# A job planner with an engine model in place of a hand-timed order, and PSUM banks given out job by job, in a fused attention and MLP-mixer kernel

## The chip, the cores and the metric

The kernel runs on one core of a Trainium2 chip. The metric is the device time of one execution in microseconds (us). A run is marked slow when it is over 1.5% above the fastest run of the same kernel, and such runs are left out of every ratio. A ratio is the mean time of one kernel's fast runs over the mean of the other's fast runs of the same rounds, so it is not quite the ratio of the medians that are quoted beside it. Brackets behind a ratio are its 95% interval.

The engines are PE (matrix multiply; PEld is its weight load), DVE (vector), ACT (activation), POOL (general) and SP, which here only issues transfers (its timelines in the traces of before and after list 60 issues each and nothing else). PE writes its results to PSUM, which this kernel uses as eight banks of 128 partitions by 512 float32. Other work that takes a bank waits until ACT or DVE has read it out: in the trace of the kernel before, PE waited for that 27 times at the attention's matmuls, 16.8 us in all.

## The reference

The inputs are drawn as float32. There are 8 batches and 8 heads, the sequence length is 1024, the head size 64.

```python
k_proj = np.einsum('ks,bhsd->bhkd', E, k)           # 1024 keys projected to 64
v_proj = np.einsum('ks,bhsd->bhkd', F, v)
attn   = softmax(q @ k_proj^T / sqrt(64))
x      = heads side by side of attn @ v_proj        # (8, 1024, 512)
# MLP-mixer:
h   = np.maximum(x^T @ w_tok1, 0) @ w_tok2          # token mixing, 1024 -> 256 -> 1024
u   = x + h^T
out = u + np.maximum(u @ w_ch1, 0) @ w_ch2          # channel mixing, 512 -> 1536 -> 512
```

(The softmax is written out in the reference, with the largest score subtracted.) Both kernels compute in bfloat16 with float32 sums.

## The kernel before

The work of a batch has two parts. The **front** is attention and token mixing: project k and v, transpose q, scores, exp on ACT, attention times v, then two token products and a transpose of u. The **channel mixing** handles each batch as two **sub-blocks** of 512 rows, 16 sub-blocks in all. It uses a seven-product scheme in the manner of Strassen for each 2 by 2 block product. A sub-block has three **up** sets of seven products of four matmuls, and one **down** block of seven products of twelve matmuls, all of 256 columns. The front of the next batch is woven between the channel products of the current one.

Each PSUM bank is a tile of its own here, from three rotating pools: three banks for up, three for down, two for the front.

```python
psU = ctx.enter_context(tc.tile_pool(name="psU", bufs=3, space=bass.MemoryType.PSUM))
psD = ctx.enter_context(tc.tile_pool(name="psD", bufs=3, space=bass.MemoryType.PSUM))
psF = ctx.enter_context(tc.tile_pool(name="psF", bufs=2, space=bass.MemoryType.PSUM))
```

The attention of a head is done in two halves, of one front bank each:

```python
def attend(b, h, half):
    o_ps = psF.tile([P, 4, D1], F32, tag="f", name="o_ps")
    for jj in range(2):
        ...                                              # one matmul of 130 columns
    rdn = attn_pool.tile([P, 4], F32, tag="rdn", name="rdn")
    nc.vector.reciprocal(out=rdn, in_=o_ps[:, :, D])
    nc.vector.tensor_tensor(
        out=xs[b][:, 4 * half : 4 * half + 4, h * D : (h + 1) * D],
        in0=o_ps[:, :, 0:D], in1=rdn[:, :, None].to_broadcast([P, 4, D]), op=ALU.mult)
```

The order comes from a list of events with times chosen by hand. All events are sorted by time and emitted in that order, and `pin()` keeps it. Note the first unit of a front, which is the place where the q transposes of the batch are issued:

```python
def front(b, begin, end):
    unit(0.0, lambda: (start_front(b), q_transpose(b)))   # two DMA transposes on SP
    unit(1.9, lambda: kv_proj(b, 0, H))
    ...
    unit(0.4, lambda: scores(0))
    if b + 1 < B:
        unit(0.0, lambda: load(b + 1, "q_sb", q, 2))      # POOL: waits until qT has read q_sb
    ...                                                   # scores, attend, token1, token2
front(1, 26, 45)
for b in range(2, B):
    front(b, 42 * b - 46 + OFF, 42 * b - 4 + OFF)
...
for _, _, f in sorted(events, key=lambda e: e[:2]):
    f()
    pin()
```

SP issues three things in the order of the program: the DMA transposes of q (qT), the DMA transposes of u (uT), and the output stores. An issue whose input is not ready holds up everything behind it: in the trace of the kernel before, one pair of uT held the queue for 20.16 us, and the store and the qT pair behind it were issued 0.1 and 0.7 us after its end.

The softmax here doesn't subtract the row's maximum and nothing guards it: scores larger than these inputs give would overflow.

Of the kernel before, what the change touches and what calls it, by code (L numbers as in the profile page):

```python
# [13 lines left out]
FMAX = 3.4028234663852886e38  # L14


@with_exitstack
def kernel(
# [13 lines left out]
    nc = tc.nc  # L32
# [36 lines left out]
    const = ctx.enter_context(tc.tile_pool(name="const", bufs=1))  # L69
    one = ctx.enter_context(tc.tile_pool(name="one", bufs=1))  # L70
    two = ctx.enter_context(tc.tile_pool(name="two", bufs=2))
    attn_pool = ctx.enter_context(tc.tile_pool(name="attn", bufs=4))
    out_pool = ctx.enter_context(tc.tile_pool(name="outp", bufs=3))
    psU = ctx.enter_context(tc.tile_pool(name="psU", bufs=3, space=bass.MemoryType.PSUM))
    psD = ctx.enter_context(tc.tile_pool(name="psD", bufs=3, space=bass.MemoryType.PSUM))
    psF = ctx.enter_context(tc.tile_pool(name="psF", bufs=2, space=bass.MemoryType.PSUM))

    seen[0] = len(nc.cur_bb.bb.instructions)

    ident = const.tile([P, P], BF16, name="ident")  # L80
    make_identity(nc, ident)
    E_sb = out_pool.tile([P, S], BF16, tag="o", name="E_sb")
    nc.gpsimd.dma_start(out=E_sb[:KP], in_=E)
    F_sb = out_pool.tile([P, S], BF16, tag="o", name="F_sb")
    nc.gpsimd.dma_start(out=F_sb[:KP], in_=F)

    loaded = {}

    def load(b, name, src, parts):
        if (b, name) not in loaded:  # L90
            loaded[b, name] = one.tile([P, H, NSI, D], BF16, tag=name, name=name)
        hn = H // parts
        for h in range(0, H, hn):
            nc.gpsimd.dma_start(
                out=loaded[b, name][:, h : h + hn],
                in_=src[b, h : h + hn].rearrange("h (p si) d -> p h si d", p=P),
            )

    for name in ("k_sb", "v_sb", "q_sb"):
        loaded[0, name] = one.tile([P, H, NSI, D], BF16, tag=name, name=name)  # L100

    def load_pair(name, src, hp):
        hs = slice(2 * hp, 2 * hp + 2)
        nc.gpsimd.dma_start(
            out=loaded[0, name][:, hs], in_=src[0, hs].rearrange("h (p si) d -> p h si d", p=P)
        )

    for hp in range(HP):
        load_pair("k_sb", k, hp)
        load_pair("v_sb", v, hp)  # L110
    for hp in range(HP):
        load_pair("q_sb", q, hp)

    wt1_sb = const.tile([P, NSI, DT], BF16, name="wt1_sb")
    nc.gpsimd.dma_start(out=wt1_sb, in_=moe_w_tok1.rearrange("(p si) t -> p si t", p=P))
    wt2_sb = const.tile([P, TC, S], BF16, name="wt2_sb")
    nc.gpsimd.dma_start(out=wt2_sb, in_=moe_w_tok2.rearrange("(tc p) s -> p tc s", p=P))

    wc1_sb = const.tile([P, 2, 2, 2, DC // 2], BF16, name="wc1_sb")
    w1_v = moe_w_ch1.rearrange("(dc p) (ch c) -> p dc ch c", p=P, ch=2)  # L120
    cw = DC // 2 // SETS
    for m in range(SETS):
        cs = slice(m * cw, (m + 1) * cw)
        for ch in range(2):
            nc.gpsimd.dma_start(
                out=wc1_sb[:, :, :, ch, cs].rearrange("p a b c -> p (a b) c"),
                in_=w1_v[:, :, ch, cs],
            )

    wc2_sb = const.tile([P, 2, C2, DM], BF16, name="wc2_sb")  # L130
    w2_v = moe_w_ch2.rearrange("(ch cc p) d -> p ch cc d", ch=2, p=P)
    for ch in range(2):
        for c in range(0, C2, 3):
            nc.gpsimd.dma_start(out=wc2_sb[:, ch, c : c + 3], in_=w2_v[:, ch, c : c + 3])


    wT1 = const.tile([P, 3, 2, DC // 2], BF16, name="wT1")
    wT2 = const.tile([P, 3, C2, DH], BF16, name="wT2")
    load(1, "k_sb", k, 2)
    load(1, "v_sb", v, 2)  # L140
    load(1, "q_sb", q, 2)

# [13 lines left out]
    def combine2(c):  # L156
        cs = slice(c, c + 3)
        combine(
            [wT2[:, n, cs] for n in range(3)],
            *(wc2_sb[:, ch, cs, dh * DH : (dh + 1) * DH] for ch in range(2) for dh in range(2)),  # L160
        )



    vb = const.tile([P, H, 2, D1], BF16, name="vb")
    kT = const.tile([P, H, 2, KP], BF16, name="kT")
    nc.vector.memset(vb, 0.0)
    nc.vector.memset(kT, 0.0)
    for half in range(2):
        nc.vector.memset(vb[half * KP : (half + 1) * KP, :, half, D:D1], 1.0)  # L170
    zero = const.tile([P, P], BF16, name="zero")
    nc.vector.memset(zero, 0.0)

    ET_sb = const.tile([P, NSI, KP], BF16, name="ET_sb")
    FT_sb = const.tile([P, NSI, KP], BF16, name="FT_sb")
    for src, dst in ((E_sb, ET_sb), (F_sb, FT_sb)):
        e_ps = psF.tile([P, NSI, KP], BF16, tag="f", name="e_ps")
        for si in range(NSI):
            nc.tensor.transpose(e_ps[:, si, :], src[:KP, si:S:NSI], ident[:KP, :KP])
        nc.vector.tensor_copy(out=dst, in_=e_ps)  # L180
    pin()

    xs, us, uTs, Ss, Gs = {}, {}, {}, {}, {}
    st = {}


    def start_front(b):
        xs[b] = one.tile([P, NSI, DM], BF16, tag="x_sb", name="x_sb")
        us[b] = two.tile([P, NSI, DM], BF16, tag="u_sb", name="u_sb")
        st["hT"] = one.tile([P, TC, DM], BF16, tag="hT_sb", name="hT_sb")  # L190
        st["qT"] = one.tile([P, H, NJ, P], BF16, tag="qT", name="qT")
        st["kp"] = one.tile([KP, H, 2, D], BF16, tag="kp_sb", name="kp_sb")

    def start_uT(b, i):
        uTs[2 * b + i] = two.tile([P, NJ, DMC, P], BF16, tag="uT", name="uT")

    def q_transpose(b):
        for h in range(0, H, H // 2):
            nc.sync.dma_start_transpose(
                out=st["qT"][:, h : h + H // 2].rearrange("p h j s -> p (h j) s"),  # L200
                in_=loaded[b, "q_sb"][:, h : h + H // 2].rearrange("p h si d -> p (h si d)"),
            )

    def q_transpose_pe(hp):
        t_ps = psU.tile([P, 2, NJ, P], BF16, tag="u", name="t_ps")
        for h in range(2):
            for j in range(NJ):
                nc.tensor.transpose(
                    t_ps[:, h, j, :],
                    loaded[0, "q_sb"][:, 2 * hp + h, 2 * j : 2 * j + 2, :].rearrange(  # L210
                        "p s d -> p (s d)"
                    ),
                    ident,
                )
        nc.vector.tensor_copy(out=st["qT"][:, 2 * hp : 2 * hp + 2], in_=t_ps)

    def kv_proj(b, h0, hn, pool=None):
        k_sb, v_sb = loaded[b, "k_sb"], loaded[b, "v_sb"]
        hs = slice(h0, h0 + hn)
        kv_ps = psF.tile([P, H, D], F32, tag="f", name="kv_ps")  # L220
        for si in range(NSI):
            a, z = si == 0, si == NSI - 1
            nc.tensor.matmul(
                kv_ps[0:KP, 0:hn], ET_sb[:, si, :], k_sb[:, hs, si, :], start=a, stop=z
            )
            nc.tensor.matmul(
                kv_ps[KP : 2 * KP, 0:hn], FT_sb[:, si, :], v_sb[:, hs, si, :], start=a, stop=z
            )
        kp = st["kp"]
        nc.vector.tensor_copy(out=kp[:, hs, 0, :], in_=kv_ps[0:KP, 0:hn])  # L230
        nc.scalar.copy(out=kp[:, hs, 1, :], in_=kv_ps[0:KP, 0:hn])
        nc.vector.tensor_copy(out=vb[KP : 2 * KP, hs, 1, 0:D], in_=kv_ps[KP : 2 * KP, 0:hn])
        nc.scalar.copy(out=vb[0:KP, hs, 0, 0:D], in_=kv_ps[KP : 2 * KP, 0:hn])

    def k_transpose(h0, hn):
        kt_ps = psF.tile([P, H, KP], F32, tag="f", name="kt_ps")
        for h in range(hn):
            nc.tensor.matmul(
                kt_ps[:, h, :], st["kp"][:, h0 + h].rearrange("k r d -> k (r d)"),
                ident[:KP, :KP], start=True, stop=True,  # L240
            )
        hs = slice(h0, h0 + hn)
        nc.vector.tensor_copy(out=kT[0:D, hs, 0, :], in_=kt_ps[0:D, 0:hn])
        nc.scalar.copy(out=kT[D : 2 * D, hs, 1, :], in_=kt_ps[D : 2 * D, 0:hn])

    def scores(h):
        s_ps = psF.tile([P, S2], F32, tag="f", name="s_ps")
        nc.tensor.matmul(  # L248
            s_ps, kT[:, h].rearrange("p c k -> p (c k)"),
            st["qT"][:, h].rearrange("p j s -> p (j s)"), start=True, stop=True,  # L250
        )
        a_sb = attn_pool.tile([P, S2], BF16, tag="a_sb", name="a_sb")
        nc.scalar.activation(out=a_sb, in_=s_ps, func=ACT.Exp, scale=scale)  # L253
        st["a", h] = a_sb
# [407 lines left out]
```

## Time and profile before

| | before |
|---|---|
| time | 615.28 us (614.71 to 615.85, 2 runs) |
| span of the profiled run | 607.4 us, mean granted clock 0.943 |
| first up product on PE | 44.7 us |
| start of sub-block 2 | 120.7 us |
| per batch, sub-blocks 2 to 15 | 69.0 us |
| from the start of sub-block 15 to the end | 38.4 us |

The last rows are read from the trace of PE by counting: a sub-block is taken to start where the 84 up matmuls of each sub-block ahead of it have been issued. (For sub-blocks 1 and 15 its own first up matmul can run 2 to 4 us before that, since neighbouring sets overlap; for sub-block 2 the two are the same.) The time per batch is the distance between the starts of sub-blocks 2 and 15, divided by 6.5.

These lines are from the page of the kernel before: span, busy time of each engine, then the busy tenths of PE and the tenths of granted clock in 40 equal slices.

```profile
span 607.4 us, 9110 instructions
PE 448.1 (74%) x3665; PEld 340.5 (56%) x3686; DVE 334.6 (55%) x784; ACT 238.2 (39%) x428; POOL 106.1 (17%) x122
PE   3787767776894679946799367993779868898785
PEclk9888988999999699997999979998789999999999
```

PE is the fullest engine and still has over a quarter of the span free. Its row has a hole (4, 4, 3, 3 in the middle) about every five slices, which is once per batch. The next lines are the waits of the same kernel: the engine and line that waited, what it waited for, and then us in total, number of waits, longest wait. SPq is SP's own queue.

```profile
SPq L447 <- POOL o_sb L468: 209.6, 10, 46.4
SPq L297 <- DVE u_sb L293: 141.7, 13, 29.9
POOL q_sb L94 <- DMA qT<-q_sb: 79.6, 4, 20.7
PE s_ps L248 <- DMA qT<-q_sb: 46.9, 5, 12.0
PE oy_ps L433 <- ACT oy_ps L428: 22.2, 15, 3.7
PE o_ps L261 <- DVE x_sb L268: 16.8, 27, 2.1
PE s_ps L248 <- DVE x_sb L268: 13.7, 17, 1.9
PE oy_ps L433 <- DVE da L463: 13.5, 14, 1.5
```

The fourth line is the hole: the scores wait up to 12.0 us for qT. The first two lines are SP's own waits: 209.6 us at output stores that were not ready and 141.7 us at uT transposes whose u was not ready. The order of the issues of SP around one hole (start, time until the end of the last issue of the group, instruction):

```profile
247.95 20.16 SPq L297 DMA_TRANSPOSE uT<-u_sb  x2
268.20 0.53 SPq L447 DMA_DIRECT2D out_dram<-o_sb  x1
268.84 8.90 SPq L199 DMA_TRANSPOSE qT<-q_sb  x2
```

Straight ahead of qT stand the two uT of the batch before, which end at 268.11 us, and one store. The same hole in the timeline of PE (start, duration, instruction, idle time before it):

```profile
265.75 0.82 PE L433 MATMUL oz_ps<-wT,G 128*128 128x256 bf16 x6
...
277.69 0.58 PE L248 MATMUL s_ps<-qT,kT 128*128 128x512 bf16 x1 [10.69 <-DMA qT<-q_sb]
278.07 1.48 PE L433 MATMUL oz_ps<-wT,G 128*128 128x256 bf16 x6
```

Six matmuls of the same kind take 0.82 us ahead of the hole and 1.48 us after it: the granted clock was 1.00 from 265 to 268 us and 0.50 from 271.4 to 281.6 us. So this wait is paid twice.

### The profile page before, as it was taken

What the parts mean: (1) busy time and instruction counts of PE and PEld (TensorE: products, weight loads), DVE (VectorE), ACT (ScalarE), POOL (GpSimd) and SP (SyncE); (2) the same over time, 40 slices, a digit from 0 to 9 for tenths busy, and PEclk for the clock granted to TensorE, in tenths of its full rate; (3) what the DMA queues carried; (4) which work ended last, traced back from release to release, by engine and by line L of the source; (5) the groups of instructions that cost most, each with busy time, mean ns of one, the idle gap of its engine ahead of it and who ended that gap; (6) DMA issues with size and microseconds to landing.
All of it is one profiled execution on the core that took longest, in us unless ns stands there. A gap on an engine that the chain in (4) does not pass through costs nothing. (4 is left out here: it accounts for less than half of the span.)

```text
span 607.4 us, 9110 instructions
## 1 busy us (share of the span) xinstructions
PE 448.1 (74%) x3665; PEld 340.5 (56%) x3686; DVE 334.6 (55%) x784; ACT 238.2 (39%) x428; POOL 106.1 (17%) x122
## 2 busy tenths in 40 slices
PE   3787767776894679946799367993779868898785
PEld 2465544564663456634566245662557646677674
DVE  2565836647573274733757337472474746665642
ACT  1335443154433343334443244432434355345441
POOL 7430040040021110211102011020200102021022
PEclk9888988999999699997999979998789999999999
DMA  9999139399019900399002990029800270114102
GB/s 149 204 204 199 27 48 161 111 156 219 2 36 160 220 37 36 36 162 218 37 36 36 171 209 36 36 38 207 172 36 35 36 174 1 71 35 105 70 30 110
DMA packets 93675, 61.67 MB, mean 102 GB/s; under 512 B 59841, under 2 KB 89025, under 8 KB 93633
## 3 DMA queue, kind: packets, MB, share of 16 engines
q0 software_dynamic: 30784, 29.63, 30.8%
q1 hardware_dynamic: 62848, 31.46, 20.8%
q8 instruction: 29, 0.48, 0.3%
q14 instruction: 14, 0.11, 0.1%
HBM read 59.24 MB, written 16.78 MB: 125 GB/s over the span
## 5 line engine op out<-in xcount | busy, mean ns | idle before, releaser
L433 PEld LDWEIGHTS <-G 128*128 128x128 bf16 x1344 | 131.8, 99 | 114.9 <-issue 90.1
L390 PEld LDWEIGHTS <-wc_sb 128*128 128x128 bf16 x768 | 74.9, 100 | 33.5 <-issue 18.8
L373 DVE CUSTOM_DVE_ANT_0 g<-gz_ps,ub 128x512 bf16<-128x512 f32 x48 | 33.0, 686 | 91.3 <-PE gz_ps L390 91.1
L248 PE MATMUL s_ps<-qT,kT 128*128 128x512 bf16 x64 | 28.0, 448 | 61.5 <-DMA qT<-q_sb 46.9
L373 DVE CUSTOM_DVE_ANT_0 G<-gz_ps,ua 128x512 bf16<-128x512 f32 x48 | 33.2, 691 | 69.9 <-ACT ua L402 69.9
L253 ACT ACTIVATE a_sb<-s_ps 128x512 bf16<-128x512 f32 x64 | 38.0, 599 | 83.6 <-PE s_ps L248 83.3
L390 PE MATMUL gx_ps<-uT,wc_sb 128*128 128x256 bf16 x384 | 58.9, 277 | 13.5 <-ACT gy_ps L416 12.4
L390 PEld LDWEIGHTS <-wT 128*128 128x128 bf16 x576 | 57.5, 101 | 18.6 <-issue 3.0
L433 PE MATMUL oy_ps<-wc_sb,G 128*128 128x256 bf16 x384 | 52.0, 272 | 13.5 <-DVE da L463 13.5
L456 POOL TENSOR_TENSOR db<-db,u_sb 128x512 f32<-128x512 f32 x16 | 18.5, 1155 | 248.3 <-ACT db L455 228.4
L390 PE MATMUL gy_ps<-St,wc_sb 128*128 128x256 bf16 x384 | 60.1, 281 | 0.6 <-ACT ua L402 0.2
L433 PE MATMUL oz_ps<-wT,G 128*128 128x256 bf16 x384 | 56.5, 287 | 1.9 <-DVE G L410 1.8
L268 DVE TENSOR_TENSOR x_sb<-o_ps,rdn 128x256 bf16<-128x256 f32 x128 | 54.3, 425 | 4.4
L396 ACT ACTIVATE G<-gx_ps 128x512 bf16<-128x512 f32 x48 | 28.7, 597 | 65.9 <-PE gx_ps L390 65.9
L433 PE MATMUL ox_ps<-wc_sb,G 128*128 128x256 bf16 x384 | 52.1, 273 | 0.0
L405 ACT ACTIVATE G<-gy_ps 128x512 bf16<-128x512 f32 x48 | 28.6, 597 | 56.4 <-PE gy_ps L390 56.3
L261 PE MATMUL o_ps<-vb,a_sb 128*128 128x130 bf16 x256 | 35.2, 230 | 20.3 <-DVE x_sb L268 16.8
L293 DVE TENSOR_TENSOR u_sb<-u_ps,x_sb 128x512 bf16<-128x512 f32 x56 | 38.3, 689 | 16.4 <-PE u_ps L289 15.8
L433 PE MATMUL oy_ps<-wT,G 128*128 128x256 bf16 x192 | 26.9, 279 | 22.2 <-ACT oy_ps L428 22.2
L261 PEld LDWEIGHTS <-a_sb 128*128 128x128 bf16 x256 | 21.4, 100 | 32.8 <-DVE x_sb L268 23.4
L468 POOL TENSOR_TENSOR o_sb<-o_sb,u_sb 128x512 f32<-128x512 f32 x16 | 18.5, 1156 | 117.5 <-ACT o_sb L467 117.5
L402 ACT COPY ua<-gy_ps 128x512 f32<-128x512 f32 x48 | 28.2, 587 | 22.1 <-PE gy_ps L390 22.0
(90 smaller groups left out, 673.5 us busy)
## 6 DMA issues: line engine op xcount, KB each, us to landing
out_dram<-o_sb SPq DMA_DIRECT2D x32, 512.0 KB, 2.9
k_sb<-in_k_dram POOLq DMA_DIRECT2D x14, 512.0 KB, 7.6
v_sb<-in_v_dram POOLq DMA_DIRECT2D x14, 512.0 KB, 12.2
q_sb<-in_q_dram POOLq DMA_DIRECT2D x14, 512.0 KB, 7.8
wc_sb<-in_moe_w_ch_dram POOLq DMA_DIRECT2D x6, 256.0 KB, 13.2
wc_sb<-in_moe_w_ch_dram POOLq DMA_DIRECT2D x4, 384.0 KB, 12.1
k_sb<-in_k_dram POOLq DMA_DIRECT2D x4, 256.0 KB, 6.4
v_sb<-in_v_dram POOLq DMA_DIRECT2D x4, 256.0 KB, 7.0
```

Source lines behind the costliest of these rows:

```text
L248: nc.tensor.matmul(s_ps, kT[:, h].rearrange("p c k -> p (c k)"), st["qT"][:, h].rearrange("p j s -> p (j s)"), start=True, stop=True,)
L253: nc.scalar.activation(out=a_sb, in_=s_ps, func=ACT.Exp, scale=scale)
L261: nc.tensor.matmul(o_ps[:, 2 * jj : 2 * jj + 2].rearrange("p c d -> p (c d)"), a_sb[:, j * P : (j + 1) * P], vb[:, h].rearrange("k c d -> ...
L268: nc.vector.tensor_tensor(out=xs[b][:, 4 * half : 4 * half + 4, h * D : (h + 1) * D], in0=o_ps[:, :, 0:D], in1=rdn[:, :, None].to_broadcas ...
L293: nc.vector.tensor_add(out=us[b][:, si, :], in0=u_ps, in1=xs[b][:, si, :])
L373: nc.vector._custom_dve(TENSOR_ADD_SAT, out=out, in0=in0, in1=in1, s0=FMAX, s1=0.0)
L390: nc.tensor.matmul(ps[:, c, :], w1_of(n, dd, 2 * m + c), a_of(j, n, dd), start=(n in (1, 7) and c == 0 and dd == 0), stop=(c == 1 and dd = ...
L396: nc.scalar.activation(out=G[:, 0, cs], in_=ps, func=ACT.Relu)
L402: nc.scalar.copy(out=up[s, "a"], in_=ps)
L405: nc.scalar.activation(out=G[:, 1, cs], in_=ps, func=ACT.Relu)
L433: nc.tensor.matmul(ps[:, t, :], Gs[j][:, G_OF[n], cc, t * P : (t + 1) * P], w2_of(n, cc), start=(n in (1, 7) and t == 0 and cc == 0), stop ...
L456: nc.gpsimd.tensor_add(out=bt, in0=bt, in1=u_of(1, 0))
```

## The change

The intent is to have the order computed instead of tuned by hand. Every piece of work becomes a job with an engine, a modelled duration, the data that it reads and writes, and the bank that it takes. A greedy list scheduler walks through modelled time: of the jobs that can start within 0.02 us of the earliest one, it takes the one with the earliest due time, and gives it a bank that is free. Up and down products may take any of six banks, the front has the other two. The diff, cut to its core:

```diff
+class Planner:
+    LAG = {"PE": 0.22, "DVE": 0.10, "ACT": 0.10, "POOL": 0.15, "SP": 0.1, "LD": 0.1}
+    ...
+        def home(b, now):                       # which bank a job would get, and when
+            if held[b.stream] + b.n > self.caps[b.stream]:
+                return None
+            ...
+            if b.n == 1:
+                spots = [(i,) for i in ((6, 7) if b.stream == "F" else range(6))]
+            else:
+                spots = [(6, 7)]                # a job of two banks needs both front banks
+    ...
+                t0 = min(c[0] for c in cands) + 0.02
+                c = min((c for c in cands if c[0] <= t0), key=lambda c: (c[1], c[2]))
...
-    psU = ctx.enter_context(tc.tile_pool(name="psU", bufs=3, space=bass.MemoryType.PSUM))
-    psD = ctx.enter_context(tc.tile_pool(name="psD", bufs=3, space=bass.MemoryType.PSUM))
-    psF = ctx.enter_context(tc.tile_pool(name="psF", bufs=2, space=bass.MemoryType.PSUM))
+    pairs = [ps.tile([P, 2, S2], F32, tag=f"ps{i}", name=f"ps{i}") for i in range(4)]
+    def bank(b):
+        t = pairs[b.at[0] // 2]
+        return t if b.n == 2 else t[:, b.at[0] % 2, :]
+    pl = Planner({"U": 3, "D": 3, "F": 2})
+    MM = {512: 0.216, 256: 0.109, 130: 0.057, 128: 0.057, 64: 0.057}
...
+    def attend(h, due):
+        bk = Bank("F", 2)                       # both front banks, four matmuls
+        ...
+            lambda: nc.vector.reciprocal(out=rdn, in_=view()[:, :, :, D]),
+        ...                                     # one multiply of 512 columns for a head
...
-        h_ps = psU.tile([P, TC, P], F32, tag="u", name="hp_ps")      # token1_pair, batch 0
+        bk = Bank("F")
-        u_ps = psD.tile([P, NJ, P], F32, tag="d", name="up_ps")      # token2_pair, batch 0
+        bk = Bank("F")
...
+        if b + 1 < B:
+            begin, end = 2 * TU * (b + 1) - 62, 2 * TU * (b + 1) - 14
+            q_transpose(begin - 15)             # due 15 us ahead of its front
+            front(b + 1, begin, end)
+    plan = pl.plan()
+    for j in plan:
+        j.fn()
+        pin()
```

## The prediction

> **What bounds it now.** The page gives PE 448.1 us busy of a 607.4 us span (74%), DVE 55%, ACT 39%. PE is the fullest engine and stands still about 159 us. At full clock the timeline shows twelve 256-column matmuls in 1.32 us (0.11 each) and 512-column ones 0.216 apart. From these I estimate the pure streaming: 2688 products x 0.11 = 296 us, and about 12.7 us of attention and token mixing for each of 8 batches, 397 us in all. So the limit is the order in which work is queued, not any engine's amount of work.
>
> The waits view names the stalls of PE: scores waiting for the DMA transpose qT, 46.9 us in five waits (longest 12.0); oy for its ACT seed 22.2 and for DVE's da 13.5; o_ps and s_ps for DVE's x_sb (bank release) 16.8 and 13.7; gx 12.4: 125 us. The qT wait is head-of-line blocking. On the SP queue, output stores waited 209.6 us for POOL's o_sb add (longest 46.4), and the qT transposes stand behind them and behind the uT transposes; POOL itself held 79.6 us at q_sb loads waiting for qT. The seven pairs of qT issues run from 55.8 to 492.3 us: 72.7 us per batch, against some 50 us of streaming.
> After a 10.7 us qT wait, six 256-column matmuls took 1.48 instead of 0.82 us: the clock had dropped[...].
>
> **What the change does.** The arithmetic, loads and the number of matmuls stay (6 more blank ones). Order and bank placement come from a list scheduler whose durations fit this trace (256 columns 0.109; DVE 512 from PSUM 0.69; ACT 0.60; POOL 1.15). The built order shows: qT of batches 1 and 2 issued before the first uT; later qT halves stand between single stores, apart from the uT pair; q loads go in halves. Up and down products take any of six banks. Attention takes both front banks at once and does one reciprocal and one multiply per head: DVE work falls from 54.3 + 22.5 us to an estimated 44 + 12, off the critical path; in exchange scores and attention of a head share two banks.
>
> **Sum (estimate).** First product at 44.7 us before; about 45 after (same loads, and DMA is full there). Remaining streaming 397 - 13 = 384, plus 8 for clock below full. Residual stalls: the qT wait (47) goes; of the other 78 about 55 to 60 stay or are replaced by new ones (a uT transpose landing late, DVE at over 70% when the period shrinks, the two front banks). 45 + 384 + 8 + 58 = 495 us: 20% faster. Most of the removed time is directly PE's, so on the critical path.
>
> **What the profile would show.** Right: qT wait on PE below 10 us; qT issues about 55 us apart; PE busy over 82%; granted clock near 0.98 with no half-clock slices after 100 us; DVE's x_sb group halved in count. First product near 45 us. Wrong if: PE waits on DMA qT or uT stay at 5 to 10 us per batch; POOL adds stuck behind loads; oy/gx seed waits grow.
>
> **What would make it wrong.** The plan fixes each queue's order from modelled DMA times; if transposes slow down beside loads (uT landed in 4.6 us median, 15.8 at most), in-order SP and POOL queues turn that into PE stalls every batch, and the gain shrinks to 560. If the plan holds nearly everywhere, 455.
>
> Chances: faster by over 2% 0.95, within 2% 0.03, slower 0.02. Predicted 495 us, range 458 to 545.

Its sum: 45 + 384 + 8 + 58 = 495 us. The 8 us are an estimate; they are 2% of the 384 and so fit the granted clock of 0.98 that the forecast expects, where before had 0.943.

## More of the kernel before

Last come the busy times in three stretches (from:to, its length, then PE, PEld, DVE, ACT, POOL with their instruction counts, granted clock, DMA share, GB/s), and one group of instructions (count | busy us, mean ns | idle before).

```profile
0.00:50.00 50.00, 32.70 (x327) 24.18 (x329) 24.22 (x69) 15.30 (x34) 23.81 (x38) 0.90 1.17 188
50.00:100.00 50.00, 34.16 (x260) 24.03 (x259) 32.97 (x77) 22.42 (x39) 6.74 (x8) 0.90 0.61 101
300.00:350.00 50.00, 34.78 (x281) 26.40 (x285) 26.99 (x58) 16.74 (x29) 6.49 (x7) 0.96 0.50 90
L268 DVE TENSOR_TENSOR x_sb<-o_ps,rdn 128x256 bf16<-128x256 f32 x128 | 54.3, 425 | 4.4
```

## The result, and the profile after

| | before | after |
|---|---|---|
| time | 615.28 us | 560.25 us (559.58 to 560.92, 2 runs) |
| ratio | | 0.9106 [0.9046, 0.9165] |
| first up product | 44.7 | 50.3 |
| start of sub-block 1 | 66.1 | 102.0 |
| start of sub-block 2 | 120.7 | 147.2 |
| per batch, sub-blocks 2 to 15 | 69.0 | 57.4 |
| from the start of sub-block 15 | 38.4 | 38.3 |
| span | 607.4 | 558.8 |

All four runs are fast ones. The steady part gains 11.6 us per batch, 75 us in 6.5 batches; the start gives 26.5 us back. The page of the kernel after:

```profile
span 558.8 us, 9128 instructions
PE 458.6 (82%) x3692; PEld 346.7 (62%) x3692; DVE 325.7 (58%) x656; ACT 234.9 (42%) x428; POOL 106.7 (19%) x122
PE   5555467888789989888888898989899889988995
PEclk8567577998799999999999999999999999999998
```

The holes are gone, but the first six slices are half empty, and the clock stands at 5 to 8 tenths there. Behind them, PE is at 8 or 9 in nearly every slice and still not full. The waits:

```profile
SPq L894 <- POOL o L901: 177.8, 14, 22.5
...
PE ps L554 <- DVE x_sb L572: 9.6, 12, 2.5
PE ps L869 <- ACT G L796: 7.5, 10, 1.7
PE ps L606 <- DVE u L617: 5.4, 15, 0.6
```

No wait of PE for qT is left; the 46.9 us of before are gone. Stores still hold SP for 177.8 us, and the qT issues still stand among them and behind a uT, but they are those of the batch after the next and so come in time. Their starts run from 56.1 to 403.6 us, that is (403.6 - 56.1) / 6 = 57.9 us per batch against 72.7. The largest PE wait that the view names is 9.6 us. So the view of waits does not explain the 100 us that PE is idle. The stretches and the group:

```profile
0.00:50.00 50.00, 26.55 (x215) 17.90 (x216) 18.22 (x45) 10.81 (x25) 23.80 (x38) 0.69 1.16 185
50.00:100.00 50.00, 31.79 (x238) 22.65 (x237) 23.58 (x49) 15.19 (x28) 4.44 (x6) 0.69 0.75 126
300.00:350.00 50.00, 44.10 (x372) 34.42 (x371) 33.74 (x68) 25.05 (x45) 9.65 (x11) 1.00 0.68 117
L572 DVE TENSOR_TENSOR x_sb<-ps,rdn 128x512 bf16<-128x512 f32 x64 | 44.2, 691 | 2.0
```

In the steady stretch PE issues 372 matmuls in 50 us where it issued 281. In the first 50 us it issues 215 where it issued 327, at a clock of 0.69 where it was 0.90. The timeline of PE shows what happens there:

```profile
50.31 0.82 PE L775 MATMUL ps<-uT,wc_sb 128*128 128x256 bf16 x4
...
55.42 0.59 PE L554 MATMUL ps<-vb,a 128*128 128x130 bf16 x4 [0.67 <-ACT uT L722]
57.10 0.59 PE L554 MATMUL ps<-vb,a 128*128 128x130 bf16 x4 [1.09 <-DVE x_sb L572]
...
61.80 0.59 PE L554 MATMUL ps<-vb,a 128*128 128x130 bf16 x4 [2.50 <-DVE x_sb L572]
63.42 3.57 PE L663 MATMUL ps<-x_sb,wt_sb 128*128 128x128 bf16 x32 [1.02 <-DVE x_sb L572]
...
73.46 1.06 PE L775 MATMUL ps<-uT,wc_sb 128*128 128x256 bf16 x4
```

The first up product (line 775) runs at 50.31 us, on half of the columns. The attention (line 554) of the last heads of batch 0 comes only at 55 to 62 us; before, the attention of batch 0 ended at 37.7 us. The second token product of those heads follows that, and the channel mixing gets going only at 73 us.

### The profile page after: what moved, and what is told of

It is laid out like the page before. It is cut to its first block, busy times and chain, and to the rows that moved or that the text cites. A ratio compares the mean times of both kernels' runs of the same rounds, so it can differ in the third digit from the quotient of the medians.

```text
span 558.8 us, 9128 instructions
## 1 busy us (share of the span) xinstructions
PE 458.6 (82%) x3692; PEld 346.7 (62%) x3692; DVE 325.7 (58%) x656; ACT 234.9 (42%) x428; POOL 106.7 (19%) x122
## 4 chain that ended last, share of the span: by engine, by line
PE 52%; DVE 20%; ACT 13%; DMA 10%; issue 4%; POOL 0%; DVEq 0%; ACTq 0%; POOLq 0%
PE ps L869 17%; PE ps L775 16%; DMA uT<-u 9%; PE ps L606 4%; PE ps L586 4%; DVE u L617 4%; DVE x_sb L572 2%; PE ps L438 2%; PE ps L533 2%; ACT ps L815 2%; DVE g L756 2%; DVE S L645 2%; ACT G L796 2%; DVE G L809 2%; DVE G L756 2%
## 5 line engine op out<-in xcount | busy, mean ns | idle before, releaser
L869 PE MATMUL ps<-wc_sb,G 128*128 128x256 bf16 x768 | 104.7, 273 | 13.0 <-ACT G L796 6.1
L796 ACT ACTIVATE G<-ps 128x512 bf16<-128x512 f32 x96 | 57.4, 598 | 100.5 <-PE ps L775 92.4
L869 PE MATMUL ps<-wT,G 128*128 128x256 bf16 x576 | 78.8, 274 | 5.5 <-ACT ps L907 1.4
L775 PE MATMUL ps<-uT,wc_sb 128*128 128x256 bf16 x384 | 59.8, 280 | 8.3 <-DVE g L756 3.5
L617 DVE TENSOR_TENSOR u<-ps,x_sb 128x512 bf16<-128x512 f32 x56 | 37.5, 689 | 42.2 <-PE ps L606 40.3
L775 PE MATMUL ps<-S,wc_sb 128*128 128x256 bf16 x384 | 58.4, 275 | 3.6 <-DVE G L756 1.9
L901 POOL TENSOR_TENSOR o<-o,u 128x512 f32<-128x512 f32 x32 | 37.1, 1160 | 123.1 <-ACT o L899 117.7
L775 PE MATMUL ps<-S,wT 128*128 128x256 bf16 x384 | 57.0, 278 | 3.8 <-ACT ps L907 1.0
L572 DVE TENSOR_TENSOR x_sb<-ps,rdn 128x512 bf16<-128x512 f32 x64 | 44.2, 691 | 2.0
L809 DVE TENSOR_TENSOR G<-G 128x512 bf16<-128x512 bf16 x96 | 43.4, 452 | 2.5
L802 ACT COPY ub<-ps 128x512 f32<-128x512 f32 x48 | 28.1, 585 | 10.9 <-PE ps L869 4.4
```

What stands on the lines that cost most here:

```text
L572: lambda: nc.vector.tensor_tensor(out=x_sb[:, :, h * D : (h + 1) * D].rearrange("p (n c) d -> p n c d", n=2), in0=view()[:, :, :, 0:D], in ...
L617: lambda: nc.vector.tensor_add(out=u_t[b % 2][:, si, :], in0=bank(bk), in1=x_sb[:, si, :]),
L775: nc.tensor.matmul(t[:, c, :], w1_of(n, dd, 2 * m + c), a_of(j, n, dd), start=(n in (1, 7) and c == 0 and dd == 0), stop=(c == 1 and dd == 1),
L796: lambda: nc.scalar.activation(out=G[:, n, cs], in_=view(src), func=ACT.Relu),
L802: 512, lambda: nc.scalar.copy(out=dst, in_=view("y")), writes=[(name, s % 2)],
L809: 512, lambda: f(out=G[:, n, cs], in0=in0, in1=in1), ps=False, reads=deps,
```

## The experiments

These are the theories. The first group says where the gain comes from; the second says what was given back.

- **Queue**: the gain is qT being issued earlier on SP, above all ahead of uT, which needs no planner. Rival: the gain is the computed order of the rest.
- **Starvation**: a job that needs both front banks never starts while jobs of one bank keep taking the bank that falls free first. Rival: it is the order of the batch-0 front, or the move of its token mixing from the up and down banks to the front banks.
- **Pair tile**: waits are kept per tile, so a tile of two banks makes work on one bank wait for work on the other. Rival: the plan itself is as good as such a plan gets, and the rest is latency.
- **Transpose model**: uT is modelled as too fast, so its readers are planned too early.

In all experiments the arithmetic is that of the kernel after, or for the b kernels that of before. The quoted expectations give the theories letters, in the order in which they came up; the paragraphs below use the names above. Each ratio is against the kernel before, run on the same chip in the same rounds. Between rounds the median of the kernel before moved from 613.8 to 616.5 us, so a difference of two experiments from different rounds is uncertain by some 3 us.

### Undoing the parts of the change one at a time

**a1_reserve**: a front job of one bank may not pass over a two-bank job that is ready and due earlier.

```diff
+                two = min(((j.prio, j.n) for j in js if j.takes and j.takes[0].n == 2), default=None)
+                        if two and j.takes[0].stream == "F" and (j.prio, j.n) > two:
+                            continue
```

> The changed kernel, with one rule added to the planner: a front job that takes one bank may not overtake a ready attention job that takes two. Theory A (starvation: in the plan single-bank jobs of a later due time keep taking the front bank that comes free, so attention of heads 4 to 7 of batch 0, which needs both at once, starts at 55 us): attention of batch 0 ends by about 47 us, the first product of subblock 1 comes at 78 to 85 us instead of 102, time about 535 to 542. Theory B (the start is bound by loads of weights and of batch 1, or by the cold clock): subblock 1 still starts at about 100 us and the time stays within 1% of 560.

Measured: 547.66 us, ratio 0.8886 [0.8846, 0.8926]. The attention of batch 0 ended (the last of its matmuls started) at 45.3 us instead of 62.1, sub-block 2 started at 140.9 instead of 147.2, and a batch took 56.2 instead of 57.4. Starvation is real and costs about 13 us. It is the smaller part of what was lost: sub-block 2 still starts 20 us later than before. (The "cold clock" of theory B is the granted clock of 0.69 that the trace of after shows in the first 100 us, against 0.90 in the trace of before.)

**a2_half_attend**: attention again in two halves of one bank each, as before; the tiles stay pairs.

```diff
-        bk = Bank("F", 2)
+        bk = Bank("F")            # one job for each half, 130 columns x 2, multiply of 256
```

> The changed kernel with attention put back into halves of one bank each, as before the change (two reciprocals and two multiplies a head). Theory A: no job needs two banks, so none starves: start as with the added rule, subblock 1 at 78 to 85 us, time 535 to 545; DVE gains 20 us of busy time without costing PE much. Theory B: start unchanged, time 560 or a little more for the added DVE work.

Measured: 565.15 us, ratio 0.9172 [0.9131, 0.9213]. The attention of batch 0 ended at 48.2 us, yet the kernel was not faster than after. No job needs two banks here, so starvation cannot be the main loss. (What halves are worth once the banks are apart is seen below.)

**a3_pairs_ud**: token mixing of batch 0 in up and down banks again.

```diff
-        bk = Bank("F")                              # token1_pair
+        bk = Bank("U")
-        bk = Bank("F")                              # token2_pair
+        bk = Bank("D" if i == 0 else "F")
```

> The changed kernel with the token mixing of batch 0 in banks of the up and down streams, as before the change, attention still in two front banks. Theory A: fewer jobs compete for the front banks, but the transposes and scores still do: attention of batch 0 ends between 45 and 60 us, time 540 to 550. Theory B: no change, within 1% of 560.

Measured: 546.38 us, ratio 0.8867 [0.8819, 0.8914], but the result is wrong (relative error 0.054). No run isolated the cause. In the program, the seed of an up bank is written by ACT, and matmuls without a start flag are to add to it; here, token mixing takes some of those banks ahead of that. All later kernels that put token mixing into these banks (h0, h1, h2, s2, s7) add one blank matmul behind it, and all are correct. That points to what token mixing leaves behind in the bank, which is the author's reading and was not tested alone. The time of this run says only that the start gets shorter with more banks to use: the attention ended at 53.9 us and sub-block 2 started at 137.8.

**a4_qt_late**: the q transposes of a batch may be issued only after the second uT of the batch before.

```diff
-                reads=[("q", i) for i in range(h, h + H // 2)],
+                reads=[("q", i) for i in range(h, h + H // 2)] + [("uT", 1, 0)],
```

> The changed kernel, the transposes of q made to follow the second uT transpose of the batch before, as they stood on the SP queue before the change. Theory C (early qT is what gained the time in the steady stretch, the planner alone gains little): 595 to 620, with PE waiting for qT or with the front stretched, some 66 us per batch. Rival D (the planner hides the late qT behind products): within 2% of 560.

Measured: 603.06 us (598.09 to 607.53, the highest one slow), ratio 0.982 [0.9738, 0.9901], a verdict of unclear between same and faster. A batch takes 64.4 us instead of 57.4. With this one property taken away, the planner's order is worth about 2%.

**b1_qt_early**: the opposite test. The kernel before, with only the issue of the q transposes moved to the point behind the last scores of the batch before.

```diff
-        unit(0.0, lambda: (start_front(b), q_transpose(b)))
+        unit(0.0, lambda: (start_front(b), q_transpose(b) if b == 1 else None))
...
+                if h + 3 == H and b + 1 < B:
+                    unit(0.0, lambda: q_transpose(b + 1))
```

> The kernel before, with one edit: the transposes of q for the next batch are issued right after the last scores of this batch, ahead of the uT transposes and stores on the SP queue. Theory C (the steady gain of the change is mostly the end of the head-of-line blocking of qT): the wait of scores for qT falls from 47 us to below 10, time 560 to 575, so about all of the net gain of the change. Rival D (the gain is the planner's finer interleaving of products, the qT wait would only be moved): the qT wait goes but other waits take its place, time 595 or more.

Measured: 560.65 us (556.41 to 562.62), ratio 0.9087 [0.9033, 0.9141]. This is the whole net gain of the change, from moving two issues. In the trace of this run qT still comes right behind a store that was waited for (17.5 us before the pair at 281.4 us), but ahead of the uT pair, and PE never waits for it. A batch takes 61.5 us instead of 69.0. The waits of PE in this run begin with these lines, and none for qT is among them:

```profile
PE oy_ps L436 <- ACT oy_ps L431: 24.5, 15, 3.7
PE o_ps L264 <- DVE x_sb L271: 16.5, 26, 2.1
PE s_ps L251 <- DVE x_sb L271: 13.7, 17, 1.9
```

They are the waits of the kernel before, nearly to the number, less the one for qT. So the planner, which also reorders everything else, adds nothing to this as built. Either its order is no better than the one by hand, or something takes its gain away again.

### The start

**h1_start** and **h0_start_nores**: the front of batch 0 is chained in the order of the kernel before, with attention in halves for batch 0 and token mixing in up and down banks, with blank matmuls behind it. h1 has the rule of a1 as well, h0 has not.

```diff
+    for f, hp in (
+        (kv0, 0), (kv0, 1), (kt0, 0), (kv0, 2), (kt0, 1), (kv0, 3), (kt0, 2), (kt0, 3),
+        (qt, 0), (qt, 1), (sc, 0), (qt, 2), (sc, 1), (att, 0), (att, 1), (qt, 3), (sc, 2),
+        (att, 2), (sc, 3), (tp, 0), (tp, 1), (att, 3), (tp, 2), (tp, 3), ...
+    ):
+        f(hp, due)                              # each PE job also writes "start": a chain
```

> The changed kernel with the added rule of a1_reserve and with the start of the kernel before inside the planner: batch 0's front in the old order (a chain of dependencies), its attention in halves of one bank, its token mixing in banks of the up and down streams. Theory A2 (what the change lost before subblock 2, 147 against 121 us, is the planner's order and banks of batch 0's front, not loads): subblock 2 starts at 120 to 127 us and the time is 522 to 535. Rival B2 (the start is set by loads or by the front of batch 1): subblock 2 stays at 137 or later, time 540 or more.

> As h1_start but without the added rule. Theory A2: subblock 2 starts as early as in h1_start; the steady stretch then shows what the rule is worth there: about 57.4 us per batch as in the changed kernel against 56.2 with the rule, so 5 to 10 us more than h1_start.

Measured: h1 552.23 us (0.9004 [0.8944, 0.9064]), h0 547.21 us (0.8934 [0.8876, 0.8991]). The attention of batch 0 still ended at about 51 us, and sub-block 2 started at 143.1 and 141.2 us. The order of before alone does not bring the start of before back, so the idea that the order at the start is the cause falls. So does the idea that the slow clock at the start is the main one: in the first 100 us, h0 ran for 20.5 us at half clock, much as before did (19.8), and still started sub-block 2 20 us later. And the rule of a1 gains nothing where batch 0 has no two-bank job: h0 is the faster of the two. What is wrong shows in the timeline of PE of h0, in the attention of batch 0:

```profile
30.02 0.27 PE L592 MATMUL ps<-vb,a 128*128 128x130 bf16 x2 [0.34 <-DVE rdn L605]
30.89 0.27 PE L592 MATMUL ps<-vb,a 128*128 128x130 bf16 x2 [0.60 <-DVE rdn L605]
31.77 0.38 PE L592 MATMUL ps<-vb,a 128*128 128x130 bf16 x2 [0.60 <-DVE rdn L605]
```

Each half needs one bank, and there are two. In s2, below, PE does write one while DVE reads the other (matmuls of one half from 26.51 to 26.78 us, the multiply of the half before from 26.58). Here it stands idle for 0.60 us instead each time, until the reciprocal of the half before, which reads the *other* bank. DVE waits in its turn; this line is from the timeline of DVE of the same run:

```profile
31.21 0.42 DVE L610 TENSOR_TENSOR x_sb<-ps,rdn 128x256 bf16<-128x256 f32 x1 [0.36 <-PE ps L592]
```

This multiply belongs to the matmuls of 30.02. Its own reciprocal ran at 30.67 us, and it still waited for the matmuls of 30.89, which write the other bank. The two engines take turns on the tile. That is the pair-tile theory, which nobody had stated in the prediction.

**h2_ut8**: h1, with uT modelled as 8 us of SP's time in place of 4 (`sp(8.0, ...)`).

> As h1_start, with the uT transposes modelled at 10 us from issue to landing instead of 6, as the trace of the changed kernel shows them beside loads (8.5 to 11 us), so that the sums that read them stand later in the order of DVE. Theory E (sums waiting for uT hold up DVE's queue and so PE): DVE's waits for uT vanish, 3 to 8 us less than h1_start. Rival: those waits have slack, the same time within 2 us.

Measured: 547.75 us, ratio 0.8945 [0.8895, 0.8995], 4.5 us less than h1 in the same rounds. The planner lets a uT land 2 us after the time that it holds SP, so 6 us after its issue, and 10 us in h2. In the kernel after, it landed after 5.7 us in the median, 4.2 at best and 11.0 at most: 6 is near the median and 10 near the worst case. (The packets of a uT, 512 KB or 128 x 2048 bf16, moved within 2.6 us at best, about 200 GB/s, so that rate alone does not give the 4.2 us.) The 4.5 us are no more than the rule of a1 moved the time here in the unexpected direction (h1 against h0, 5.0), so the transpose model is a small term at most.

### Banks as tiles of their own

A static count was made first. In each built program, every wait on an engine's semaphore (its own included, transfers left out) was traced to the instruction at which it ends. It was counted as "other bank" when the two share no data and no bank, only the PSUM tile:

| kernel | waits | of these: other bank of the tile |
|---|---|---|
| before | 2149 | 0 |
| after | 1832 | 586 |
| a2_half_attend | 1956 | 809 |
| s1_six | 1729 | 181 |
| s5_half_six | 1853 | 426 |
| s4_half_eight | 1973 | 0 |

A recount from the kernels gave the same totals, and the right column within 2%. Not each of these waits would vanish without the pair: some would be replaced by an earlier wait that is needed. What they cost has to be measured.

**s1_six**: the kernel after, same plan and same instructions in the same order, but the six up and down banks are six tiles. The front pair stays, since its attention writes both banks.

```diff
-    pairs = [ps.tile([P, 2, S2], F32, tag=f"ps{i}", name=f"ps{i}") for i in range(4)]
+    single = [ps.tile([P, S2], F32, tag=f"ps{i}", name=f"ps{i}") for i in range(6)]
+    front_pair = ps.tile([P, 2, S2], F32, tag="psF", name="psF")
```

> The changed kernel with the six banks of the up and down streams as six tiles instead of three tiles of two banks each (the front's two banks stay one tile). Theory F (a tile of two banks makes the jobs of its two banks wait for each other, though they share no data): the stretch from subblock 2 to 15 falls from 57.4 us per batch to 53 to 56, PE's waits for ACT G and DVE g shrink, time 535 to 552; the start, in the front's banks, stays (subblock 2 at about 145 us). Rival (waits are tracked bank by bank, the tiles do not matter): the same time within 1% of 560.

Measured: 513.16 us, ratio 0.8392 [0.8322, 0.8462]: 47 us less than after, from the way in which the same memory is declared. A batch takes 51.5 us instead of 57.4.

**s4_half_eight**: a2, the same plan as there, with eight tiles of one bank each (`for i in range(8)`).

> a2_half_attend (attention in halves) with all eight banks tiles of their own. Theory F: a2_half_attend was slow (565) since the halves waited for each other inside the front's tile; now 530 to 548. Rival (halves cost by their DVE work): 558 or more.

**s5_half_six**: the same with six tiles and the front pair kept.

> Attention in halves and the six tiles for the up and down streams, the two front banks still one tile. Between a2_half_attend (565) and s4_half_eight (478) it splits the gain. If the shared front tile is what made halves slow: 505 to 525, at least 25 us over s4_half_eight. If splitting the six was all of it and halves help by themselves: within 5 us of 478.

Measured: s4 478.33 us (0.7818 [0.7757, 0.788]) and s5 522.9 us (0.852 [0.8459, 0.8582]), where a2 took 565.15. With one and the same plan, six tiles are worth 42 us and the split of the front pair another 45. The page of s4 and its steady stretch:

```profile
span 475.5 us, 9211 instructions
PE 432.6 (91%) x3692; PEld 342.7 (72%) x3692; DVE 331.0 (70%) x784; ACT 235.6 (50%) x428; POOL 107.2 (23%) x122
300.00:350.00 50.00, 47.72 (x414) 38.04 (x412) 36.39 (x90) 27.15 (x49) 9.97 (x10) 1.00 0.62 128
```

PE now issues 414 matmuls in the stretch where after had 372 and before 281. Halving the attention, which gained nothing in a2, is right as soon as the banks are apart: s4 beats s1 by 35 us, although DVE does more and smaller instructions (784 instead of 656).

The waits that were removed are not needed by the hardware as far as these runs go: all three kernels (s1, s4, s5) give correct results.

**b2_single** and **b2_pairs**: the reverse control, with no planner in it. In b1, the three pools are replaced by a small class that hands out fixed banks in rotation (up 0 to 2, down 3 to 5, front 6 and 7). In b2_single, a bank is a tile; in b2_pairs, it is half of a tile. Nothing else differs.

```diff
-    single = [ps.tile([P, S2], F32, tag=f"ps{i}", name=f"ps{i}") for i in range(8)]
-    at_bank = lambda i: single[i][:, :]
+    pairs = [ps.tile([P, 2, S2], F32, tag=f"ps{i}", name=f"ps{i}") for i in range(4)]
+    at_bank = lambda i: pairs[i // 2][:, i % 2, :]
```

> Control: b1_qt_early (the kernel before with q's transposes early) with its eight banks as eight lasting tiles that the same three streams use in turn, in place of tiles from pools. Expected: within 1.5% of b1_qt_early, 555 to 569, since each bank is still a tile of its own.

> The reverse of the cure: b2_single with the same banks in the same turns, but two banks to a tile, as the changed kernel has them; order and arithmetic are untouched. Theory F: slower than b2_single by 20 to 60 us, since halves of attention, and up and down products that share a tile, wait for each other. Rival (tiles do not matter, the gain of s1 and s4 came of another plan): the same time within 1%.

Measured: b2_single 557.8 us (0.9087 [0.9018, 0.9157]), as b1. b2_pairs 775.28 us (1.2652 [1.2536, 1.2768]). The pairs alone cost 217 us. The waits of PE in b2_single:

```profile
PE ps L459 <- ACT ps L454: 24.6, 15, 3.7
PE ps L287 <- DVE x_sb L294: 19.2, 29, 2.1
...
PE ps L459 <- DVE da L489: 12.2, 13, 1.5
```

And in b2_pairs:

```profile
PE ps L287 <- DVE x_sb L294: 62.1, 59, 2.9
PE ps L416 <- ACT ps L442: 31.1, 26, 2.2
PE ps L416 <- DVE da L489: 23.4, 14, 2.5
```

The last line is the plainest proof. Line 416 is an up product. Line 489 is DVE's reading of a finished down product into `da`. They share no data and no bank. In b2_single the only wait of PE for `da` is at line 459, a down product that follows in the same bank; in b2_pairs an up product waits for it 14 times, because its bank is the other half of the tile.

### Combinations

**s2_start_eight**: h0 with all attention in halves and eight tiles. **s3_res_six**: s1 with the rule of a1.

> As h0_start_nores (the old start inside the planner), with all attention in halves of one bank and all eight banks tiles of their own. Theory F: the halves of attention no longer wait for each other (in h0_start_nores the second half waited for the reciprocal of the first, in the other bank), attention of batch 0 ends by 40 us instead of 51, subblock 2 starts at 121 to 130 us, time 515 to 530. Rival: the start stays at 141, time 540 or more.

> The rule of a1_reserve and the six tiles of s1_six together. If the two causes are separate their gains add: 13 us from the rule and what s1_six shows, so 525 to 540. If both only shift the same wait: no better than the better of the two.

These two scattered: s2 gave 472.42, 480.25, 481.31 and 488.35 us, s3 503.47, 511.03, 511.68 and 514.1. In each, only the first counts as fast, so there is no ratio, and the difference between s3 and s1 stays inconclusive. One reading of s2 is safe, since the difference is large: its sub-block 2 starts at 113.4 us, where h0 started it at 141.2. The order of before at the start does work, once the pairs are gone. The same attention as shown for h0 above, in the timeline of PE of s2:

```profile
26.51 0.27 PE L562 MATMUL ps<-vb,a 128*128 128x130 bf16 x2 [0.31 <-DVE x_sb L580]
27.06 0.27 PE L562 MATMUL ps<-vb,a 128*128 128x130 bf16 x2 [0.28 <-DVE x_sb L580]
```

A half now comes every 0.55 us instead of every 0.88. PE waits for the multiply that frees its own bank, and DVE is busy without a gap: in its timeline the multiply (0.42 us) and the reciprocal (0.17 us) follow each other at once.

**s7_start_ut8**: s2 with uT modelled as 8 us.

> The best so far carried on: s2_start_eight with the uT transposes modelled at 10 us from issue to landing. If uT's landing still holds up queues (s2's chain of waits has uT at 8%): 465 to 476; if not, 470 to 488 as s2_start_eight.

Measured: 469.79 us (464.3 to 471.43, the highest one slow), ratio 0.7616 [0.7536, 0.7696], correct. It is the fastest kernel: 24% less than before, 16% less than after. Its span is 468.7 us, PE is busy for 91% of it, sub-block 2 starts at 120.1 us and a batch takes 48.2 us.

**s6_eight_qt_late**: s4 with the late q transposes of a4.

> s4_half_eight (478 us) with q's transposes made late as in a4_qt_late. If the late transposes are a limit of their own: about as in a4_qt_late, 25 to 45 us more, 503 to 525. If, with the false waits gone, the front has room for them: below 490.

Measured: 500.51 us, ratio 0.815 [0.8095, 0.8204]: 22 us more than s4. The early q transposes are worth 56 us in the order by hand (b1), 43 in the kernel after (a4) and 22 with the banks apart. The worth of one cure depends on what else is standing still. (In the traces of a4 and s6, SP issues the uT pair, a store and then qT, as in the kernel before.)

### The sum of the evidence

The expectations had the pair tiles too small throughout: s1 was expected at 535 us or more (513.16 measured), s4 at 530 or more (478.33), s2 at 515 or more (472.42 to 488.35), and the cost in b2_pairs at 20 to 60 us (217). The cure of starvation was expected too large: 535 to 542 us for a1 (547.66), 535 to 545 for a2 (565.15).

| order, with qT early | banks apart | banks in pairs | cost of the pairs |
|---|---|---|---|
| by hand (b2_single, b2_pairs) | 558 | 775 | 217 |
| planner, halves (s4, a2) | 478 | 565 | 87 |
| planner, attention over two banks (s1, after) | 513 (six banks apart, front pair kept) | 560 | 47 |

Read down the first column: the planner's order with halves is better than the one by hand by 79 us (557.8 - 478.3). Read across: the pairs take all of that away. The kernel after has both, and ends where the kernel before ends with two issues moved. What inside the planner's order makes the 79 us (the free choice among six banks, the finer order, or the order of the loads) was not taken apart and stays open.

## Why the prediction was wrong

The direction and much of the mechanism were right; the time, 560.25 us, is outside the range of 458 to 545.

What held:
- "the qT wait (47) goes": no PE wait for qT is left. b1 shows that this was a cause of time and not only a line in a list. (What stood right ahead of qT was uT, which the prediction names second, and not the stores, which it names first.)
- "qT issues about 55 us apart": 57.9. "PE busy over 82%": 82%. "DVE's x_sb group halved in count": 64 instead of 128, and the estimates of 44 and 12 us measured 44.2 and 13.0.
- The clock, in part. That matmuls were slow after the wait of 10.69 us holds (1.48 us instead of 0.82, at a granted clock of 0.50 instead of 1.00). The start of after has half clock without such a wait: in the first 100 us the granted clock was 0.69, with half clock for 61 us, though no idle stretch of PE was longer than 2.9 us. What sets the clock there stays open. Of "granted clock near 0.98 with no half-clock slices after 100 us" the second half held nearly (10 us at half clock between 132 and 153 us, and the last 3 us); the mean was 0.933, for the most part through those 61 us at the start.

What failed, term by term, with the profiled spans:

| term | predicted | measured |
|---|---|---|
| start of sub-block 2 | 45 + 2 x 28.1 = 101 | 147.2 |
| 6.5 batches | 6.5 x 56.3 = 366 | 373.4 |
| from sub-block 15 to the end | 28 | 38.3 |
| sum | 495 | 558.8 |

(The prediction's 450 us behind the first product were one flow; divided by 16 sub-blocks they are 28.1 us each.)

1. **The step that failed most is "First product at 44.7 us before; about 45 after", with the streaming put right behind it.** The first product did come at 50.3 us. But it was no sign of streaming: sub-block 1 followed only at 102.0 us, and the start was 46 us longer than predicted. The runs put two causes in its place. Waits of one bank for its neighbour are the larger: with the same plan as a2, s4 starts sub-block 2 at 118.2 us instead of 149.1. Starvation of the two-bank attention is the smaller: a1 gains 13 us in all, 6 of them at the start. A third part stays open: in the best kernels (s2, s4, s7) sub-block 2 still starts at 113 to 120 us, 12 to 19 later than 101, about where the kernel before had it (120.7). No run shows what holds it there.
2. **"in exchange scores and attention of a head share two banks" was seen and costed at nothing.** Going back to halves, with the front banks apart as well, is worth 35 us once the other banks are apart (s4 against s1); how this divides between the two-bank job and the front tile was not measured.
3. **"Residual stalls: ... about 55 to 60 stay or are replaced by new ones" came out nearly right, for a wrong reason.** The steady batches took 57.4 us where 56.3 were predicted. The plan with halves leaves far less: 49.5 us per batch in s4, where the streaming was estimated at 397 / 8 = 49.6. The stalls that filled the difference are mostly the false waits of the pair tiles: with the six up and down banks apart alone (s1), a batch takes 51.5 us. The near hit is luck: had the steady part been the only one, the right number would have hidden a missing cause.
4. **The end was spread evenly over the sub-blocks.** From the start of sub-block 15 there is no front left to fill the gaps. It took 38.4 us before, 38.3 after and 35.2 in the best kernels, so a look at the timeline of before would have given it.
5. "If transposes slow down beside loads ... the gain shrinks to 560" named the measured number by luck, with another cause. The test of it (h2 against h1) is worth 4.5 us.

With the false waits cured, the plan does what the prediction expected of it: 478 us in s4 and 470 in s7 lie in the range.

## What to carry to other kernels

When a kernel hands out memory by its own plan, declare it in the same pieces that the plan hands out: in these builds the tile is what waits are kept for, so two banks in one tile are one resource, however well the plan spreads the work (217 us between b2_pairs and b2_single, 87 between a2 and s4). Before writing a scheduler, look in the order of the issuing queues for a transfer that is not ready with something urgent right behind it, and do not take the longest wait in the list for the harmful one; here, moving two issues per batch was worth 9%. And in a greedy plan, a job that needs two resources at once starves behind jobs that need one (about 13 us here, a1): split it, or hold the resource for it.
